# Idle matmuls in the planned waits of TensorE, new task ranks, later weights and last stores by SyncE, in a kernel of gated attention and an MLP

## The chip, the cores and the metric

One core of one Trainium2 chip. The metric is device time in microseconds (us) of one execution of the program, as a median of repeated runs. Engines: PE is TensorE, DVE is VectorE, ACT is ScalarE, POOL is GpSimd, SP is SyncE. The profile's span is counted from the first to the last instruction and is some 1.8 us shorter than the timed run it belongs to.

## The reference

```python
f = 1 / (1 + exp(-f_logit))                      # q, k, v, f_logit: 4 x 8 x 768 x 48, float32
for t in range(S):
    state = f[:, :, t, :, None] * state + k[t] outer v[t]
    y[:, :, t] = q[:, :, t] @ state
x = y as (3072 tokens, 384)
h = x @ w_in                                     # 384 x 2048
out = (h * sigmoid(h)) @ w_out                   # 2048 x 384
```

The kernel works in 24 units: 12 half-chunks m of 128 time steps and two of the four batches, each with two units j. A unit has an attention part (written m.j below) and an MLP part.

## The kernel before

The kernel does not write its instructions in a fixed loop. A small planner inside it holds a list of tasks, each with an engine, an assumed duration, the tasks it needs, a rank and the buffers it takes. It simulates the engines, and the order that comes out is the order in which the instructions are written. Each engine's instruction stream then has that order, with semaphores where the data cross engines. So a constant of the planner can change the order of all five engines. The tasks of a unit, shortened:

```python
add(n("L"),  "ACT", 0.95, logs, ...)          # log of the gate (two ACTIVATEs)
add(n("cs"), "PE",  0.165, cumsum, ...)       # running sum
add(n("ia"), "ACT", 0.4, inverse, ...); add(n("aa"), "ACT", 0.4, forward, ...)
add(n("ki"), "POOL", 1.0, scale_k, ...); add(n("qg"), "DVE", 0.95, scale_q, ...)
add(n("T"),  "PE",  0.45, transposes, ...);  add(n("qk"), "DVE", 0.65, transposed, ...)
add(n("A"),  "PE",  0.34, scores, ...);      add(n("am"), "DVE", 1.25, masked, ...)
add(n("Y"),  "PE",  0.37, outputs, ...);     add(n("yc"), "DVE", 0.5, output_copy, ...)
add(n("D"),  "PE",  0.18, update, ...);      add(n("st"), "DVE", 1.1, state, ...)
add(n("X"),  "PE",  0.17, turn, ...);        add(n("xT"), "DVE", 0.35, turned, ...)
# ... MLP: I (into the hidden layer, PE), S (silu, ACT), O (out, PE), R (copy, ACT), G (store, POOL)
SPLIT = (0, 1, 2)            # half-chunks whose MLP is done per unit, 128 columns a matmul, not 256
BEFORE = {0: ["ki1.0"]}      # the eight weight transfers, issued by POOL, wait for this task
```

The weights are converted from float32 on the way, and POOL issues their transfers. The idle matmuls multiply zeros into an MLP bank of PSUM:

```python
def warm():
    w_ps = hps.tile([128, 2 * HT], F32, name="w_ps", tag="h_ps")
    nc.tensor.matmul(w_ps[:, 0:NP * 2 * D], zeros[:, 0:128], zeros, start=True, stop=True)
# in the planner, before the start of a PE task, while the first MLP task is still to come:
    while start - at > 0.6:
        self.order.append((at, filler)); at += 0.165 if at > 4.5 else 0.33
```

## Time and profile before

| what | before |
|---|---|
| time, median | 204.23 us (203.98 to 205.19, 3 runs) |
| span of the profiled execution | 203.2 us |
| first MLP matmul | 22.25 us |
| PE idle, from there to the last matmul | 6.95 us |
| clock: time lost from there on, (1 - granted clock) x length | 3.3 us (over 60 to 90 us; 3.4 with the rounding of 70 to 78 us) |
| last matmul to the end of the span | 5.1 us |

The last three rows, with the 15.7 us of idle time and idle matmuls before the first MLP matmul, are the budget that the argument uses: time in which PE does nothing useful at full clock. In a stretch of the windows view, idle is length less PE's busy time. The prediction below shows the lines and works the budget out. The profiled execution took 204.98 us.

### The profile page before, as it was taken

The numbers are of one execution on the slowest core, as the hardware profiler recorded it, in microseconds if no ns is written. First come the engines' busy times: TensorE is split into PE (matmuls) and PEld (weight loads), VectorE is DVE, ScalarE is ACT, GpSimd is POOL, SyncE is SP. The second block draws the span as 40 slices with busy tenths as digits, with TensorE's granted clock in tenths as the row PEclk, the third lists the DMA queues.
The fourth block names the chain that finished last, engine by engine and source line by source line (L and its number), as shares of the span: only waits on it lengthen the run. The fifth ranks groups of instructions, "written<-read, shape, count | busy, mean of one in ns | idle before, by whom it ended". The sixth has DMA issues, their size and how long they took to land.

```text
span 203.2 us, 5048 instructions
## 1 busy us (share of the span) xinstructions
PE 186.7 (92%) x2076; PEld 139.1 (68%) x2076; DVE 112.5 (55%) x214; ACT 130.6 (64%) x244; POOL 59.0 (29%) x90
## 2 busy tenths in 40 slices
PE   7788899997999489979999999999999999999990
PEld 3445799554876258658768888667778889865650
DVE  3478650048784956589989940399999750000000
ACT  4446488646898664987798779996346568911110
POOL 5339600135241421192047110473520000012221
PEclk9979999999999959999999999999999999999999
DMA  7999999999999999999999997021110000002111
GB/s 133 187 187 167 170 188 184 197 194 286 189 184 209 214 182 188 180 225 217 175 198 220 205 176 110 2 79 42 39 54 27 3 0 3 0 30 75 68 69 71
DMA packets 105110, 27.06 MB, mean 133 GB/s; under 512 B 100352, under 2 KB 103936, under 8 KB 105088
## 3 DMA queue, kind: packets, MB, share of 16 engines
q1 hardware_dynamic: 99840, 18.88, 58.5%
q0 software_dynamic: 5248, 7.87, 16.2%
q8 instruction: 16, 0.26, 0.6%
q14 instruction: 6, 0.05, 0.1%
HBM read 25.17 MB, written 4.72 MB: 147 GB/s over the span
## 4 chain that ended last, share of the span: by engine, by line
PE 37%; issue 27%; DMA 12%; SPq 9%; DVE 7%; POOL 4%; ACT 2%; POOLq 0%; DVEq 0%; ACTq 0%
PE h_ps L403 14%; DMA q_ld<-in_q_dram 11%; PE o_ps L418 10%; SPq L227 9%; PE t_ps L312 3%; POOL out_dram L432 3%; PE h_ps L388 2%; PE a_ps L324 2%; DVE st L379 2%; DMA f_ld<-in_f_logit_dram 2%; DVE qg L288 2%; POOL ki L285 1%; PE y_ps L344 1%; DVE sd L376 1%; PE y_ps L340 1%
## 5 line engine op out<-in xcount | busy, mean ns | idle before, releaser
L418 PE MATMUL o_ps<-w_out_sb,hT 128*128 128x384 bf16 x384 | 68.4, 326 | 0.4 <-DMA w_out_sb<-in_moe_w_out_dram 0.4
L403 PE MATMUL h_ps<-xT,w_in_sb 128*128 128x256 bf16 x432 | 53.5, 279 | 0.0
L412 ACT ACTIVATE hT<-h_ps 128x512 bf16<-128x512 f32 x72 | 42.8, 597 | 16.3 <-PE h_ps L403 13.7
L418 PEld LDWEIGHTS <-hT 128*128 128x128 bf16 x384 | 36.0, 98 | 22.1 <-issue 0.6
L403 PEld LDWEIGHTS <-w_in_sb 128*128 128x128 bf16 x432 | 41.5, 100 | 6.0 <-issue 0.2
L285 POOL TENSOR_TENSOR ki<-k_ld,ia 128x384 bf16<-128x384 f32 x24 | 24.4, 1018 | 53.5 <-ACT ia L277 41.3
L288 DVE TENSOR_TENSOR qg<-q_ld,a 128x384 bf16<-128x384 f32 x24 | 21.3, 886 | 29.9 <-ACT a L282 18.8
L331 DVE TENSOR_TENSOR atm<-a_ps,triu 128x512 bf16<-128x512 f32 x48 | 30.9, 684 | 7.2 <-PE a_ps L324 6.9
L432 POOL DMA_DIRECT2D out_dram<-o_sb x24 | 13.6, 567 | 57.5 <-ACT o_sb L424 55.1
L424 ACT COPY o_sb<-o_ps 128x384 f32<-128x384 f32 x24 | 11.4, 477 | 23.4 <-PE o_ps L418 23.4
L291 POOL CAST vb<-v_ld 128x384 bf16<-128x384 f32 x22 | 12.9, 593 | 28.8 <-DMA v_ld<-in_v_dram 19.8
L277 ACT ACTIVATE ia<-cs 128x384 f32<-128x384 f32 x24 | 11.8, 492 | 11.4 <-PE cs L272 11.4
L388 PE MATMUL h_ps<-xT,w_in_sb 128*128 128x128 bf16 x288 | 17.7, 219 | 1.3 <-DVE xT L362 0.8
L317 DVE COPY qk<-t_ps 128x1024 bf16<-128x1024 bf16 x24 | 16.4, 682 | 4.4 <-PE t_ps L312 4.4
L258 ACT ACT_TABLE_LOAD x14 | 18.0, 1283 | 1.0 <-PEq L560 0.7
L388 PEld LDWEIGHTS <-w_in_sb 128*128 128x128 bf16 x288 | 16.4, 98 | 2.0 <-issue 1.0
L396 ACT ACTIVATE hT<-h_ps 128x512 bf16<-128x512 f32 x24 | 14.0, 597 | 5.1 <-PE h_ps L388 4.1
L351 DVE CAST y<-y_ps 128x384 bf16<-128x384 f32 x24 | 13.3, 554 | 7.2 <-PE y_ps L344 6.9
L265 ACT ACTIVATE f_ld<-f_ld 128x384 f32<-128x384 f32 x24 | 12.5, 522 | 6.1 <-DMA f_ld<-in_f_logit_dram 6.1
L379 DVE TENSOR_TENSOR st<-sd,al 48x192 bf16<-48x192 f32 x32 | 13.6, 425 | 0.8
L312 PE MATMUL t_ps<-ident,qg 128*128 128x128 bf16 x96 | 9.8, 226 | 3.6 <-DVE qg L288 3.5
L266 ACT ACTIVATE lf<-f_ld 128x384 bf16<-128x384 f32 x24 | 12.5, 523 | 0.8
(41 smaller groups left out, 182.2 us busy)
## 6 DMA issues: line engine op xcount, KB each, us to landing
f_ld<-in_f_logit_dram SPq DMA_DIRECT2D x24, 192.0 KB, 4.5
k_ld<-in_k_dram SPq DMA_DIRECT2D x24, 192.0 KB, 4.6
q_ld<-in_q_dram SPq DMA_DIRECT2D x24, 192.0 KB, 4.5
v_ld<-in_v_dram SPq DMA_DIRECT2D x24, 192.0 KB, 4.7
out_dram<-o_sb POOLq DMA_DIRECT2D x24, 192.0 KB, 2.2
w_in_sb<-in_moe_w_in_dram POOLq DMA_DIRECT2D x4, 384.0 KB, 8.3
w_out_sb<-in_moe_w_out_dram POOLq DMA_DIRECT2D x4, 384.0 KB, 16.4
```

The costliest lines, as they stand in the source:

```text
L227: nc.sync.dma_start(out=t, in_=src)
L258: nc.scalar.preload_act_table_set(tables[name])
L285: nc.gpsimd.tensor_mul(ki[m % 4][:, j, :, 0:D], loaded[m, j, "k"], ias[m, j])
L288: nc.vector.tensor_mul(qg[m % 4][:, j, :, 0:D], loaded[m, j, "q"], aas[m, j])
L317: nc.vector.tensor_copy(qkT[m, j], t_ps[m, j])
L331: nc.vector.tensor_mul(atm[m, j][:, r], att[m, j][:, r], triu[:, None, :].to_broadcast([C, NP, C]))
L379: nc.vector.tensor_mul(st[b][lo:lo + D, :, r * D:(r + 1) * D], src[lo:lo + D, :, r * D:(r + 1) * D], alast[m][lo:lo + D, j, :, None].to_br ...
L388: nc.tensor.matmul(h_ps[:, i], w_in_sb[:, kk, (n + i) * 128:(n + i + 1) * 128], xT[m][:, kk, j], start=(kk == 0), stop=(kk == KT - 1))
L403: nc.tensor.matmul(h_ps[:, i], w_in_sb[:, kk, (n + i) * 128:(n + i + 1) * 128], xT[m][:, kk].rearrange("p b c -> p (b c)"), start=(kk == 0 ...
L412: nc.scalar.activation(hT[m][:, n:n + 2, :], hs[m, n], AF.Silu)
L418: nc.tensor.matmul(os[m, j], hT[m][:, i, j * C:(j + 1) * C], w_out_sb[:, i, :], start=(i == 0), stop=(i == NT - 1))
L432: eng.dma_start(out=out[r0:r0 + C, :], in_=osb[m, j])
```

## The change

The intent is to leave PE without a gap in the plan and to put idle matmuls where a gap remains, so that the clock isn't lowered. The core of the diff:

```diff
-            if e == "PE" and filler is not None and until in left:
+            if e == "PE" and filler is not None:
-                while start - at > 0.6:
+                size, taken = self.pools["h"]
+                while start - at > self.slack:              # slack = 0.4
+                    if len(taken) >= size:
+                        if taken[-size] not in self.freed or self.freed[taken[-size]] > at:
+                            break
                     self.order.append((at, filler))
-    patience = 0.7
+    patience = 2.2
...
-        eng = {"ACT": nc.scalar, "POOL": nc.gpsimd, "SP": nc.sync}[STORE]      # STORE = "POOL"
+        eng = nc.sync if m >= LATE else nc.gpsimd                              # LATE = 8
...
-    SPLIT = (0, 1, 2)
+    SPLIT = (1, 2)
-    BEFORE = {0: ["ki1.0"]}
+    BEFORE = {0: ["ki1.1"], 4: ["ki1.1"]}
...
-            add(n("L"), "ACT", 0.95, ..., rank=r + 5)       # r = m * 10 + j * 3
+            add(n("L"), "ACT", 1.05, ..., rank=base + W["L"])    # base = m * 7 + j * 4
...          # 19 ranks in all, of the attention tasks
-            add(n("qk"), "DVE", 0.65, ...)
+            add(n("qk"), "DVE", 0.68, ...)
-                add(n("D"), "PE", 0.18, ...)
+                add(n("D"), "PE", 0.26, ...)
```

The entry 4 of `BEFORE` adds nothing, as each weight transfer waits for the one before it. Three assumed durations change with the ranks.

More of the change, by code (lines that the diff above doesn't have):

```diff
@@ L72, in pool_ready, with run @@
         return ready
-    def run(self, filler=None, until=None):
+    def run(self, filler=None):
         tasks, end, self.freed = self.tasks, {}, {}
@@ L131, in run @@
                 continue
-            if e == "PE" and filler is not None and until in left:
+            if e == "PE" and filler is not None:
                 at = max(free.get(e, 0.0), 1.0)
-                while start - at > 0.6:
+                size, taken = self.pools["h"]
[3 more added lines that the diff above has]
+                            break
                     self.order.append((at, filler))
                     at += 0.165 if at > 4.5 else 0.33
+                    taken.append(f"warm{at}")
+                    self.freed[f"warm{at}"] = at + 0.2
             if swap:
@@ L176, in allowed @@
         return True
-    patience = 0.7
+    patience = 2.2
+    slack = 0.4
     def emit(self):
@@ L422, in result @@
         osb[m, j] = wk.tile([C, d_model], F32, name="o_sb", bufs=4)
-        if COPY == "ACT":
-            nc.scalar.copy(osb[m, j], os[m, j])
-        else:
-            nc.vector.tensor_copy(osb[m, j], os[m, j])
+        nc.scalar.copy(osb[m, j], os[m, j])
     def store(m, j):
@@ L446, in do @@
         return lambda: fn(*args)
-    COPY, STORE = "ACT", "POOL"
-    SPLIT = (0, 1, 2)
+    W = dict(m=7, j=4, L=1, cs=-2, ia=-9, aa=4, ki=3, qg=1, vb=0, T=5, qk=4, A=3, am=1, Y=14,
+             yc=1, D=13, st=1, X=1, xT=-3, al=5, ea=-1)
+    LATE = 8
+    SPLIT = (1, 2)
     WRANK = -10
-    BEFORE = {0: ["ki1.0"]}
+    BEFORE = {0: ["ki1.1"], 4: ["ki1.1"]}
     units = [(m, j) for m in range(NH) for j in range(HB)]
@@ L464 @@
         g = m // 2
-        add(f"al{m}", "PE", 0.2, do(totals, m), [U("L", m, j) for j in range(HB)], rank=m * 10 + 9, takes="yd", opens=1)
-        add(f"ea{m}", "ACT", 0.18, do(decay_all, m), [f"al{m}"], rank=m * 10 + 1, table="exp", frees=[f"al{m}"], opens=-1)
+        add(f"al{m}", "PE", 0.2, do(totals, m), [U("L", m, j) for j in range(HB)], rank=m * W["m"] + W["al"], takes="yd", opens=1)
+        add(f"ea{m}", "ACT", 0.18, do(decay_all, m), [f"al{m}"], rank=m * W["m"] + W["ea"], table="exp", frees=[f"al{m}"], opens=-1)
         for j in range(HB):
@@ L469 @@
             n = lambda what, mm=m: U(what, mm, j)
-            r = m * 10 + j * 3
+            base = m * W["m"] + j * W["j"]
             back = m >= 4
-            add(n("L"), "ACT", 0.95, do(logs, m, j), [n("f")] + ([n("cs", m - 4), f"al{m - 4}"] if back else []),
-                rank=r + 5, table="exp")
-            add(n("cs"), "PE", 0.165, do(cumsum, m, j), [n("L")], rank=r, takes="yd", opens=1)
-            add(n("ia"), "ACT", 0.4, do(inverse, m, j), [n("cs")], rank=r, table="exp", takes="ia")
@@ L476 @@
-            add(n("aa"), "ACT", 0.4, do(forward, m, j), [n("cs"), n("ia")], rank=r + 1, table="exp", takes="aa", frees=[n("cs")], opens=-1)
+            add(n("L"), "ACT", 1.05, do(logs, m, j), [n("f")] + ([n("cs", m - 4), f"al{m - 4}"] if back else []),
+                rank=base + W["L"], table="exp")
+            add(n("cs"), "PE", 0.165, do(cumsum, m, j), [n("L")], rank=base + W["cs"], takes="yd", opens=1)
+            add(n("ia"), "ACT", 0.4, do(inverse, m, j), [n("cs")], rank=base + W["ia"], table="exp", takes="ia")
@@ L477 @@
+            add(n("aa"), "ACT", 0.4, do(forward, m, j), [n("cs"), n("ia")], rank=base + W["aa"], table="exp", takes="aa", frees=[n("cs")], opens=-1)
             add(n("ki"), "POOL", 1.0, do(scale_k, m, j), [n("ia"), n("k")] + ([n("T", m - 4), n("D", m - 4)] if back and m - 4 < NH - 2 else []),
-                rank=r, frees=[n("ia")])
+                rank=base + W["ki"], frees=[n("ia")])
             add(n("qg"), "DVE", 0.95, do(scale_q, m, j), [n("aa"), n("q")] + ([n("T", m - 4)] if back else []),
-                rank=r + 6, frees=[n("aa")])
+                rank=base + W["qg"], frees=[n("aa")])
@@ L481 @@
             on_act = m == 1
             add(n("vb"), "ACT" if on_act else "POOL", 0.75, do(values_act if on_act else values, m, j), [n("v")] + ([n("Y", m - 4), n("D", m - 4)] if back and m - 4 < NH - 2 else []),
-                rank=r + 1)
-            add(n("T"), "PE", 0.45, do(transposes, m, j), [n("qg"), n("ki")], rank=r + 5, takes="t")
-            add(n("qk"), "DVE", 0.65, do(transposed, m, j), [n("T")], rank=r + 4, takes="qk", frees=[n("T")])
-            add(n("A"), "PE", 0.34, do(scores, m, j), [n("qk")], rank=r + 3, takes="a")
@@ L487 @@
-            add(n("am"), "DVE", 1.25, do(masked, m, j), [n("A")], rank=r + 3, takes="atm", frees=[n("A")])
+                rank=base + W["vb"])
+            add(n("T"), "PE", 0.45, do(transposes, m, j), [n("qg"), n("ki")], rank=base + W["T"], takes="t")
+            add(n("qk"), "DVE", 0.68, do(transposed, m, j), [n("T")], rank=base + W["qk"], takes="qk", frees=[n("T")])
+            add(n("A"), "PE", 0.34, do(scores, m, j), [n("qk")], rank=base + W["A"], takes="a")
+            add(n("am"), "DVE", 1.25, do(masked, m, j), [n("A")], rank=base + W["am"], takes="atm", frees=[n("A")])
@@ L488 @@
             add(n("Y"), "PE", 0.37, do(outputs, m, j), [n("am"), n("vb")] + ([n("st", m - 2)] if m >= 2 else []),
-                rank=r + 2, takes="yd", frees=[n("qk"), n("am")])
-            add(n("yc"), "DVE", 0.5, do(output_copy, m, j), [n("Y")], rank=r + 1, takes="y", frees=[n("Y")])
+                rank=base + W["Y"], takes="yd", frees=[n("qk"), n("am")])
+            add(n("yc"), "DVE", 0.5, do(output_copy, m, j), [n("Y")], rank=base + W["yc"], takes="y", frees=[n("Y")])
             if m < NH - 2:
-                add(n("D"), "PE", 0.18, do(update, m, j), [n("ki"), n("vb"), n("Y"), f"ea{m}"] + ([n("st", m - 2)] if m >= 2 else []),
-                    rank=r + 4, takes="yd")
-                add(n("st"), "DVE", 1.1 if m >= 2 else 0.72, do(state, m, j), [n("D"), n("Y"), f"ea{m}"], rank=r + 3, frees=[n("D")])
@@ L495 @@
-            add(n("X"), "PE", 0.17, do(turn, m, j), [n("yc")], rank=r + 1, takes="yd", frees=[n("yc")])
-            add(n("xT"), "DVE", 0.35, do(turned, m, j), [n("X")], rank=r, frees=[n("X")], takes="xT" if j == 0 else None)
+                add(n("D"), "PE", 0.26, do(update, m, j), [n("ki"), n("vb"), n("Y"), f"ea{m}"] + ([n("st", m - 2)] if m >= 2 else []),
+                    rank=base + W["D"], takes="yd")
+                add(n("st"), "DVE", 1.1 if m >= 2 else 0.72, do(state, m, j), [n("D"), n("Y"), f"ea{m}"], rank=base + W["st"], frees=[n("D")])
@@ L498 @@
+            add(n("X"), "PE", 0.17, do(turn, m, j), [n("yc")], rank=base + W["X"], takes="yd", frees=[n("yc")])
+            add(n("xT"), "DVE", 0.35, do(turned, m, j), [n("X")], rank=base + W["xT"], frees=[n("X")], takes="xT" if j == 0 else None)
         if m in SPLIT:
@@ L521 @@
                     frees=[owner] if n == NT - 4 and j == HB - 1 else None)
-            add(f"R{m}.{j}", COPY, 0.5 if COPY == "ACT" else 0.55, do(result, m, j), [f"O{m}.{j}.{NT - 4}"], rank=-500.0, frees=[f"O{m}.{j}.0"])
-            add(f"G{m}.{j}", STORE, 0.37 if STORE == "ACT" else 0.85, do(store, m, j), [f"R{m}.{j}"], rank=-501.0)
+            add(f"R{m}.{j}", "ACT", 0.5, do(result, m, j), [f"O{m}.{j}.{NT - 4}"], rank=-500.0, frees=[f"O{m}.{j}.0"])
+            add(f"G{m}.{j}", *(("SP", 0.05) if m >= LATE else ("POOL", 0.85)), do(store, m, j), [f"R{m}.{j}"], rank=-501.0)
             add(f"W{m}.{j}", "DMA", 0.6, None, [f"G{m}.{j}"], rank=-1)
@@ L542 @@
         for _ in range(6):
-            plan.run(warm, "I0.0.0" if 0 in SPLIT else "I0.0")
+            plan.run(warm)
             plan.transfers()
```

## The prediction

> **What bounds the kernel now.** I read the engine shares and the 40 slices of the page first, then a table of busy time in stretches cut at the events I found, then the waits of PE after its first MLP matmul, then single stretches of the timeline.
>
> ```profile
> PE 186.7 (92%) x2076; PEld 139.1 (68%) x2076; DVE 112.5 (55%) x214; ACT 130.6 (64%) x244; POOL 59.0 (29%) x90
> ...
> PE   7788899997999489979999999999999999999990
> ...
> PEclk9979999999999959999999999999999999999999
> ```
>
> PE is the bound, but not evenly: the second half is solid and every hole lies in the first 91 us. The clock row has two dips, in the third slice and around the fifteenth. The stretches (PE busy is the first number after the length, the granted clock the seventh field):
>
> ```profile
> 0.00:22.25 22.25, 17.76 (x155) 9.90 (x155) 14.16 (x37) 10.78 (x21) 12.90 (x25) 0.92 1.22 168
> 22.25:41.00 18.75, 18.40 (x262) 15.64 (x263) 4.45 (x11) 13.16 (x22) 2.45 (x3) 1.00 1.23 186
> 41.00:60.00 19.00, 17.30 (x226) 12.57 (x225) 14.13 (x24) 13.93 (x27) 7.57 (x12) 1.00 1.05 213
> 60.00:70.00 10.00, 7.18 (x100) 5.37 (x98) 7.05 (x11) 7.70 (x15) 3.60 (x6) 1.00 1.19 214
> 70.00:78.00 8.00, 7.26 (x63) 5.04 (x61) 4.65 (x10) 4.96 (x9) 1.50 (x2) 0.57 1.07 186
> 78.00:91.00 13.00, 11.69 (x137) 8.42 (x134) 9.42 (x17) 11.06 (x23) 5.66 (x9) 1.00 1.18 194
> 91.00:198.10 107.10, 107.07 (x1153) 82.17 (x1150) 58.65 (x111) 68.53 (x128) 24.82 (x35) 1.00 0.43 86
> 198.10:203.20 5.10, 0.00 (x0) 0.00 (x0) 0.00 (x0) 0.48 (x1) 0.54 (x1) 1.00 0.20 76
> ```
>
> From 91 us on PE is never idle at full clock, so whatever is saved earlier moves the end almost one for one. This gives a budget of the time in which PE does nothing useful at full speed. (a) Before the first MLP matmul at 22.25 us: 4.49 us idle (22.25 - 17.76) and 11.2 us of idle matmuls (the row of line 437), 15.7 us. (b) From 22.25 to 198.1 us: idle 0.35 + 1.70 + 2.82 + 0.74 + 1.31 + 0.03 = 6.95 us. (c) In 70 to 78 us the clock is 0.57, which costs 8.0 x 0.43 = 3.4 us. (d) The tail after the last matmul, 5.1 us. The rest, 203.2 - 31.2 = 172 us, is real work that the change leaves alone.
>
> The holes of (b) have these releasers (waited for: us in total, times, longest):
>
> ```profile
> PE t_ps L312 <- DVE qg L288: 2.5, 2, 2.1
> PE a_ps L324 <- DVE qk L317: 1.3, 1, 1.3
> PE h_ps L388 <- DVE xT L362: 0.8, 1, 0.8
> PE al_ps L300 <- DVE xT L362: 0.7, 1, 0.7
> PE y_ps L340 <- DVE sd L376: 0.6, 1, 0.6
> ```
>
> All are VectorE results of the attention part. VectorE is late because it stood still from 30 to 41 us for want of data:
>
> ```profile
> 40.93 0.56 DVE L288 TENSOR_TENSOR qg<-q_ld,a 128x384 bf16<-128x384 f32 x1 [10.79 <-DMA q_ld<-in_q_dram]
> ```
>
> That q load was issued at 19.35 us and landed 21.5 us later (the median is 4.5): the eight weight transfers, issued by POOL from 16.42 us, took the DMA engines. Afterwards VectorE is only just ahead of PE until 91 us.
>
> **What the Trainium skill says.** "TensorE: Matmul & The Clock Gate", Part 1, states that TensorE runs at half clock until it has been busy for a window of about 3.4 us and falls back after an idle one. The trace agrees: PE is idle for 2.71 of the 4 us between 66 and 70 us, and microsecond slices show 0.50 from 71 to 77, some two windows. "SBUF — State Buffer", Who interferes with whom, states that a VectorE operation with two SBUF inputs and a GpSimd operation block each other. The scaling of q is of that kind, and the trace agrees: 0.54 us at best, 1.90 at worst, here while POOL ran. "ScalarE: Activation LUTs", What ACT_TABLE_LOAD costs, gives about 1283 ns; the trace has 14 at a mean of 1283 ns. "DMA: Bandwidth & Descriptors", Latency and other measured facts, gives a first byte after about 0.6 us for transfers issued by SP and about 1 us for those by POOL; the kernel before has no store issued by SP to compare.
>
> **The change part by part.**
> (1) Idle matmuls no longer stop at the first MLP matmul; they fill every planned PE wait above 0.4 us (before: 0.6) wherever an MLP bank is free in the plan. At full clock one takes about 0.16 us (in the MLP output group, four of the same width take 0.65). They do no work and save none of the idle time itself; they keep the clock. If the holes of (b) are where the plan expects them, the 3.4 us of (c) go. They can also hold a real matmul back by up to one piece each, 0.1 us on average; I allow for five such places, +0.5. As holes stay that the plan does not know, I count -3.0 of the 3.4.
> (2) Weights wait for the key scaling of the last unit of the second chunk (ki1.1) and no longer for ki1.0. In the trace ki1.1 ran at 22.67 only because POOL was issuing weights; its input was there at 19.37. So it ends near 20.4, and the first weight issue moves from 16.42 to about 20.4. The first MLP matmul came 5.8 us after that issue and waited for that weight, so it moves from 22.25 to about 26.2, or +4.0. Meanwhile PE does real work it had to do anyway, the rest of unit 1.1: transposes 0.45, scores 0.33, outputs 0.37, update 0.18, two turns 0.34, about 1.7. Net +2.3. In return four more loads, at 1.0 us each, land at the full rate before the weights take over: one whole unit. VectorE can then work on unit 2.0 while PE does the first 21 us of MLP (4 units of 2.6 + 2.6 us), instead of standing still.
> (3) New ranks and a patience of 2.2 us for changing between the two MLP halves (before 0.7): better order, fewer table loads, and longer planned waits that idle matmuls paper over. Together with (2) this attacks the 6.95 us of (b). Rough supply check: VectorE needs 112.5/24 = 4.7 us a unit, PE 172/24 = 7.2. With one unit in hand VectorE should hardly be caught again. I count 60%, -4.2.
> (4) Stores of the last four chunks go from POOL to SP, which has been idle since 122.4 us. The last store is issued 0.29 us after the copy and takes 0.54 on POOL; POOL is otherwise free there. Only the last store counts: -0.6, an estimate from the 0.54 and the skill's two latencies.
> (5) The first chunk's MLP is no longer split: 256 columns for 128. Twelve narrow matmuls take 0.67 and six wide ones 0.65, so nothing to gain but ScalarE's order.
> Sum: 204.23 + 0.5 - 3.0 + 2.3 - 4.2 - 0.6 = 199.2. I lower it to 198.5: part (2) can cost less, because a warm PE also shortens the attention of the first chunks (in 12.6 to 15.4 us the clock is 0.5 and a scores group takes 0.61 in place of 0.40), so ki1.1 can come sooner.
>
> **Rivals.**
> A: The new order closes nearly all holes. Then (b) and (c) go wholly, 10.3 us, against 2.3 for the late weights and 0.6 at the tail: 195.6. For it: VectorE has 45% idle and 91 to 198 us shows that a full PE is possible. Against it: the plan uses fixed durations, and VectorE's vary from 0.54 to 1.90 us.
> B: The late weights cost as much as they give. The PE order is fixed, so each surprise of a neighbour makes a hole as before; only the clock is kept. Then 204.2 + 0.5 - 3.0 + 2.3 - 1.5 - 0.6 = 201.9. For it: the new ranks come from the plan, whose old ranks also promised fewer holes than the trace shows.
> C: Idle matmuls delay real ones, or wait for a bank that ScalarE has not emptied, and patience leaves real work standing. Forty extra ones of 0.16 us on the path would be 6.4 us and bring 205. Against it: they go only into planned gaps and banks planned free, and any MLP matmul that came next would need a bank too.
>
> **Range and chances.** I predict 198.5 us, between the sum and rival A, with 8 in 10 from 195.0 to 202.3: A at the low end, B within it near the top. Two per cent is at 200.1 us. I give 0.72 to faster, 0.25 to the same, where B or half of B holds, and 0.03 to slower, which needs C.
>
> **What would show it.** (1) Granted clock 1.00 in every slice after the first 16 us; a dip at 60 to 80 us would refute it. (2) First weight issue near 20.4 and first MLP matmul near 26 us; VectorE at work between 27 and 40 us on the third chunk. (3) Real idle time plus idle matmuls after the first MLP matmul under 4 us; if it is 6 or more, the order gained nothing. (4) Last store to end of span under 4 us. The prediction fails if idle matmuls after 26 us outnumber about 30 while PE waits for VectorE as long as before, or if the first MLP matmul is later than 28 us.

## The result and the profile after

The changed kernel took 199.51 us (198.49 to 199.79, 4 runs) against 204.71 us (203.98 to 205.21, 4 runs) for the kernel before; the ratio is 0.974, with a 95% interval of 0.9689 to 0.9791. Ratios here and below are the mean time of one kernel's fast runs over that of the kernel before in fast runs of the same rounds, so they are not quite the ratio of the medians. A second measurement (e12) gave 199.47 us and 0.9757.

From the page of the changed kernel, PE's busy time, the slices of PE and the clock:

```profile
PE 186.5 (94%) x2047; PEld 137.6 (70%) x2047; DVE 112.6 (57%) x214; ACT 128.4 (65%) x242; POOL 55.6 (28%) x82
...
PE   7989879999999999999999989999999999999993
...
PEclk9999999999999999999999999999999999999999
```

Both dips of the clock are gone (the early one is missing in e7 too, so its absence here proves nothing), and the slices after the start are nearly solid. The windows view of the changed kernel, cut at its own first and last MLP matmul (length, PE busy, ..., granted clock, DMA share, GB/s):

```profile
0.00:27.04 27.04, 22.09 (x206) 12.32 (x206) 19.14 (x46) 13.32 (x26) 15.00 (x27) 1.00 1.07 168
27.04:60.00 32.96, 32.46 (x389) 25.31 (x390) 13.45 (x26) 22.43 (x43) 8.71 (x13) 1.00 1.14 197
60.00:70.00 10.00, 9.34 (x143) 7.51 (x141) 8.58 (x17) 8.46 (x15) 2.99 (x6) 1.00 1.01 209
70.00:78.00 8.00, 8.00 (x103) 6.58 (x101) 4.71 (x10) 6.98 (x11) 1.63 (x3) 1.00 1.01 199
78.00:91.00 13.00, 12.77 (x152) 9.61 (x151) 11.04 (x19) 11.95 (x25) 7.39 (x9) 1.00 1.10 206
91.00:194.55 103.55, 101.87 (x1068) 76.31 (x1063) 55.70 (x100) 64.81 (x124) 19.87 (x27) 1.00 0.44 91
194.55:197.90 3.35, 0.00 (x0) 0.00 (x0) 0.00 (x0) 0.48 (x1) 0.00 (x0) 0.98 0.16 61
```

The holes from the first MLP matmul on add up to 0.50 + 0.66 + 0.00 + 0.23 + 1.68 = 3.07 us, against 6.95. The clock loss of 3.4 us is gone, and the tail is 3.35 in place of 5.1. Against that stands the start. Idle time plus idle matmuls before the first MLP matmul were 4.49 + 11.21 = 15.7 us and are now 4.95 + 14.78 = 19.7. The sum, -3.9 - 3.4 - 1.8 + 4.0 = -5.1, compares with the spans' 197.9 - 203.2 = -5.3.

So far this reads like the prediction coming true. The view of the idle matmuls themselves does not (duration in ns, first and last start in us):

```profile
L442 PE MATMUL w_ps<-zeros x63: 322/326/527, 1.1 to 24.7; 128*128 128x384 bf16 x63
```

All 63 lie before the first MLP matmul. Where the clock dip and the holes had been, not one idle matmul runs. The new plan has holes of 0.6 us in all after the first MLP matmul and none above the limit of 0.4, so the new rule finds nothing to fill. I built the changed kernel once with the old limit "only before the first MLP task": all five instruction streams come out the same, instruction for instruction. The part that names the change is empty after 25 us. Something else removed the dip.

### The profile page after: what moved, and what is told of

Same layout as the page of the kernel before. It is cut to its first block, busy times and chain, and to the rows that moved or that the text cites. A ratio compares the mean times of both kernels' runs of the same rounds, so it can differ in the third digit from the quotient of the medians.

```text
span 197.9 us, 4992 instructions
## 1 busy us (share of the span) xinstructions
PE 186.5 (94%) x2047; PEld 137.6 (70%) x2047; DVE 112.6 (57%) x214; ACT 128.4 (65%) x242; POOL 55.6 (28%) x82
## 4 chain that ended last, share of the span: by engine, by line
PE 58%; SPq 23%; DVE 10%; DMA 4%; ACT 2%; issue 1%; ACTq 0%
PE o_ps L426 23%; SPq L235 23%; PE h_ps L411 21%; DMA f_ld<-in_f_logit_dram 4%; PE t_ps L320 3%; DVE atm L339 3%; PE a_ps L332 2%; DVE st L387 2%; DVE qg L296 2%; PE h_ps L396 1%; PE cs L280 1%; PE x_ps L365 1%; DVE y L359 1%; PE y_ps L352 1%; PE y_ps L348 1%
## 5 line engine op out<-in xcount | busy, mean ns | idle before, releaser
L411 PE MATMUL h_ps<-xT,w_in_sb 128*128 128x256 bf16 x480 | 57.5, 273 | 1.4 <-DMA w_in_sb<-in_moe_w_in_dram 1.3
L420 ACT ACTIVATE hT<-h_ps 128x512 bf16<-128x512 f32 x80 | 47.3, 597 | 15.2 <-PE h_ps L411 12.3
L411 PEld LDWEIGHTS <-w_in_sb 128*128 128x128 bf16 x480 | 45.4, 98 | 7.5 <-DMA w_in_sb<-in_moe_w_in_dram 1.4
L426 PEld LDWEIGHTS <-hT 128*128 128x128 bf16 x384 | 35.7, 98 | 20.9 <-issue 0.4
L296 DVE TENSOR_TENSOR qg<-q_ld,a 128x384 bf16<-128x384 f32 x24 | 23.5, 981 | 26.8 <-ACT a L290 25.2
L442 PE MATMUL w_ps<-zeros 128*128 128x384 bf16 x63 | 14.8, 377 | 1.1 <-DVE zeros L541 1.1
L437 POOL DMA_DIRECT2D out_dram<-o_sb x16 | 9.3, 580 | 17.3 <-ACT o_sb L431 14.7
L352 PE MATMUL y_ps<-vb,atm 128*128 128x48 bf16 x192 | 12.2, 184 | 1.1 <-DVE atm L339 0.7
L396 PE MATMUL h_ps<-xT,w_in_sb 128*128 128x128 bf16 x192 | 11.9, 219 | 0.6 <-ACT hT L404 0.6
L352 PEld LDWEIGHTS <-atm 128*128 128x128 bf16 x192 | 9.8, 96 | 3.4 <-DVE atm L339 2.5
L387 DVE TENSOR_TENSOR st<-sd,al 48x192 bf16<-48x192 f32 x32 | 11.5, 360 | 0.8
```

The lines of the kernel that those rows point to most:

```text
L296: nc.vector.tensor_mul(qg[m % 4][:, j, :, 0:D], loaded[m, j, "q"], aas[m, j])
L352: nc.tensor.matmul(y_ps[:, 2 * p + r, :], atm[m, j][:, r, p, :], vb[m % 4][:, j, 2 * p + r, :], start=not opened, stop=True, skip_group_ch ...
L387: nc.vector.tensor_mul(st[b][lo:lo + D, :, r * D:(r + 1) * D], src[lo:lo + D, :, r * D:(r + 1) * D], alast[m][lo:lo + D, j, :, None].to_br ...
L411: nc.tensor.matmul(h_ps[:, i], w_in_sb[:, kk, (n + i) * 128:(n + i + 1) * 128], xT[m][:, kk].rearrange("p b c -> p (b c)"), start=(kk == 0 ...
L420: nc.scalar.activation(hT[m][:, n:n + 2, :], hs[m, n], AF.Silu)
L426: nc.tensor.matmul(os[m, j], hT[m][:, i, j * C:(j + 1) * C], w_out_sb[:, i, :], start=(i == 0), stop=(i == NT - 1))
```

## The experiments

Two theories went in. **Order**: a better order, and first of all the later weights, removes the long holes, and the clock only falls where such a hole is. **Idle matmuls**: they carry the gain, by the clock. The table has what each run left; the profile's numbers are those of its profiled execution. "Holes" is PE idle from the first MLP matmul to the last matmul.

| run | median, us | ratio to before | first MLP matmul | holes | idle matmuls in there, busy us | clock loss in there | tail |
|---|---|---|---|---|---|---|---|
| before | 204.7 | 1 | 22.25 | 6.9 | 0 | 3.3 | 5.1 |
| changed | 199.5 | 0.974 | 27.04 | 3.1 | 0 | 0 | 3.4 |
| e1 late weights only | 204.3 | 1.0013 | 26.09 | 6.0 | 0 | 0 | 5.2 |
| e2 changed, no idle matmuls after 5 us | 199.2 | 0.9768 | 26.42 | 1.8 | 0 | 1.3 | 3.4 |
| e3 changed, all stores by POOL | 200.9 | 0.9838 | 26.67 | 2.5 | 0 | 0 | 5.2 |
| e4 before, new idle matmul rule | 202.7 | 0.9927 | 21.26 | 5.9 | 3.2 | 0 | 5.1 |
| e5 changed, early weights | 203.5 | 0.9937 | 21.62 | 8.3 | 3.3 | 0 | 3.4 |
| e6 changed, old ranks | 199.1 | 0.9711 | 26.86 | 2.6 | 1.8 | 0 | 3.4 |
| e7 before, last stores by SP | 203.3 | 0.9917 | 22.10 | 7.0 | 0 | 3.3 | 3.3 |
| e8 before, new rule up to first MLP task | 205.7 | 1.0038 | 21.35 | 7.7 | 0 | 3.3 | 5.1 |
| e9 e6 with first chunk split | 200.7 | 0.9817 | 27.13 | 4.5 | 0.5 | 0 | 3.4 |
| e10 e6 with old durations | 202.2 | 0.9881 | 26.56 | 4.7 | 2.0 | 0 | 3.3 |
| e11 e6, no idle matmuls after 5 us | 200.0 | 0.9772 | profile slow | | | | |
| e12 changed again | 199.5 | 0.9757 | 26.54 | 2.6 | 0 | 0 | 3.3 |

Results were correct in all twelve runs. e1 to e4 ran on one chip, e5 to e8 on another, e9 to e12 on a third, each against runs of the kernel before on the same chip (medians 204.3, 205.0 and 204.3 us).

### e1: late weights alone

```diff
-    BEFORE = {0: ["ki1.0"]}          # in the kernel before
+    BEFORE = {0: ["ki1.1"]}
```

> The kernel before with one word changed: the weights wait for the key scaling of the last unit of chunk two, as in the changed kernel. Theory Order (the later weights fill the holes after 40 us by letting VectorE start one unit earlier, and with the holes the clock dip goes): first MLP matmul near 26 to 27 us, idle from there to the last matmul at most 4 us, no clock below 0.9 after 30 us, 199.5 to 201.5 us. Theory Idle matmuls (they are what keeps the clock, the order matters little): a dip of the clock remains after 60 us and the time is 203 or more, since the start alone costs 2 us.

204.3 us, ratio 1.0013 (0.9985 to 1.004). Both theories miss. The dip of the clock went, as Order said, but 6.0 us of holes stayed; they only moved. From the windows view of e1, its worst stretch:

```profile
100.00:110.00 10.00, 7.29 (x100) 5.54 (x99) 7.45 (x13) 7.22 (x14) 4.65 (x7) 1.00 1.17 206
```

That stretch was solid before (10.00 of 10 us busy). The timeline of ACT shows one cause: at 100.11 us the gate's logs start after 2.33 us of waiting for a load. The later weights alone gained nothing.

### e2: the changed kernel without idle matmuls

```diff
-                while start - at > self.slack:
+                while start - at > self.slack and at < 5.0:
```

> The changed kernel with its idle matmuls cut to the 14 before 5 us; everything else in the same order. Theory Order: the holes after the first MLP matmul stay as small, but the clock is half at some point between 10 and 30 us and up to 2 us are lost there: 199.5 to 201.5. Theory Idle matmuls: most of the gain goes, 202.5 or more.

199.2 us, ratio 0.9768 (0.9735 to 0.9802), against 0.974 and 0.9757 for the changed kernel: the same, and a little under the 199.5 us at which Order began. Its clock row is the striking one:

```profile
PEclk9855559999999999999999999999999999999999
```

From 8.4 to 28.9 us PE runs at half clock, and nothing is lost. The first MLP matmul comes at 26.42 us, if anything sooner than the 27.04 of the profile with all idle matmuls (26.54 in the second one). The start is paced by loads, with a gate load every 4.2 us, and by the weights, on which PE waits in the changed kernel:

```profile
27.04 1.16 PE L411 MATMUL h_ps<-xT,w_in_sb 128*128 128x256 bf16 x9 [1.28 <-DMA w_in_sb<-in_moe_w_in_dram]
```

### e3: all stores by POOL

```diff
-    LATE = 8
+    LATE = 99
```

> The changed kernel with all stores issued by POOL. The order of PE, VectorE and ScalarE is the same. If the tail is what the store's issuer makes it: the tail from the last matmul to the end of the span goes from 3.35 back to about 5.1 us and the time is 0.7 to 1.8 us longer than the changed kernel. If the tail was shorter for another cause, the time is within 0.4 us.

200.9 us, ratio 0.9838 (0.9808 to 0.9868). The streams of PE, DVE and ACT are the same as in the changed kernel, so the 1% between 0.9838 and 0.974 is the stores. The tail is 5.2 us again. This profile also says that idle matmuls don't guarantee the clock: with all 63 of them PE was idle for 2.23 of the 4 us from 17 on, and the clock was 0.50 from 21 to 24 us. Windows view of e3:

```profile
17.00:21.00 4.00, 1.77 (x22) 1.00 (x22) 1.95 (x4) 2.67 (x7) 1.46 (x2) 0.99 0.87 163
21.00:24.00 3.00, 2.99 (x31) 2.26 (x31) 2.41 (x5) 0.87 (x2) 3.00 (x5) 0.50 1.05 175
```

### e4 and e8: the idle matmul rule alone, in the kernel before

e4 takes the first two hunks of the diff (rule and slack) and leaves weights, ranks, durations and stores alone. Here the rule has holes to fill: 70 idle matmuls, 14 of them after the first MLP matmul. e8 is e4 with the old limit:

```diff
-            if e == "PE" and filler is not None:
+            if e == "PE" and filler is not None and "I0.0.0" in left:
```

> The kernel before with the new rule for idle matmuls alone: 70 in place of 44, of which the plan puts 14 after the first MLP matmul. Theory Idle matmuls: the clock dip after 70 us goes and the time falls by 3 us or more, to 201.3 or less. Theory Order: the real holes at 66 to 70 us come from VectorE and are longer than planned; the time stays within 1.5 us of the kernel before, 203 to 205, and the clock still dips there or PE waits as long.

> The kernel before with the new rule for idle matmuls only up to the first MLP matmul: 56 in place of 44, none later. The run with all 70 had 202.7 us, its first MLP matmul 1.0 us sooner and no clock dip after 70 us. If the gain came from the warm start: the same 202.4 to 203.2. If it came from the 14 later ones, which keep the clock: first MLP matmul near 21.3, but the dip at 70 us is back and the time is 203.3 to 204.5.

e4: 202.7 us, ratio 0.9927 (0.9897 to 0.9958; one of its four runs slow and left out). e8: 205.7 us, ratio 1.0038 (0.9995 to 1.0081), a little slower than the 204.5 us at which I put its upper end. Both bring the first MLP matmul 0.9 to 1.0 us forward. Why is not shown. It isn't the clock: e7, with the PE order and the idle matmuls of the kernel before, had the full clock in its start too, issued its first weights sooner (15.40 us, against 15.96 in e4 and 15.65 in e8), and still had its first MLP matmul at 22.10:

```profile
0.00:22.10 22.10, 16.47 (x155) 9.22 (x155) 14.67 (x38) 10.89 (x21) 13.76 (x26) 1.00 1.18 171
```

e8 shows that this start gains nothing: what PE begins sooner it waits for later, holes 7.7. The dip at 70 us is in e8 and not in e4:

```profile
70.00:78.00 8.00, 7.22 (x60) 5.03 (x58) 4.97 (x10) 4.73 (x9) 1.83 (x3) 0.57 0.94 184
70.00:78.00 8.00, 7.21 (x95) 5.50 (x93) 6.28 (x12) 5.42 (x11) 1.50 (x2) 1.00 0.98 186
```

The first line is e8, the second e4. So in the old order the rule without its old limit is worth about 1.1% (0.9927 against 1.0038), and it works as meant, by the clock. One rival can't be shut out entirely. The rule books an MLP bank for each idle matmul, so e4 differs from e8 by more than the 14: built again, the two plans place a dozen PE tasks, nearly all of the MLP, in another order between 24 and 48 us. But the holes up to 60 us are no smaller in e4 (3.5 us, against 2.7 in e8), so the gain doesn't come from there. Both theories missed e4: Order had it at 203 or more, Idle matmuls at 201.3 or less. It is the changed order that leaves them no work.

### e5 and e6: which of order's two parts

```diff
# e5, in the changed kernel
-    BEFORE = {0: ["ki1.1"], 4: ["ki1.1"]}
+    BEFORE = {0: ["ki1.0"]}
# e6, in the changed kernel: all 19 ranks as before, durations as changed
-                rank=base + W["L"], table="exp")
+                rank=r + 5, table="exp")
...
```

> The changed kernel with the weights again after ki1.0, everything else as changed (12 idle matmuls then fall after the first MLP matmul by plan). First MLP matmul near 21 to 22 us. Theory Pair (neither the ranks nor the late weights gain alone; together they do): holes of 5 us or more return after 40 us, and with the stores on SP the time is 201.5 to 203.5 us. Rival Ranks (the new ranks carry it, the weights' place doesn't matter): 199 to 200.5.

> The changed kernel with the old ranks (weights late, idle matmuls, stores on SP, first chunk not split as changed). Theory Pair: as the run with late weights alone less what the stores gave, 204.3 - 1.5 = 202.8, between 202 and 203.6 us, with holes of 5 us or more after the first MLP matmul. Rival Weights (late weights carry it and something else spoilt that run): under 201.

e5: 203.5 us, ratio 0.9937 (0.9888 to 0.9985), no better than the stores alone (e7). With early weights the new ranks have holes of 8.3 us. e6: 199.1 us, ratio 0.9711 (0.9659 to 0.9762), as fast as the changed kernel. I had expected 202 to 203.6. The theory that ranks and weights are a pair falls: the re-chosen ranks gain nothing that the old ones don't. The late weights are needed (e5, with the new ranks), but e1 had them too, and stood at 1.0013. What e6 has and e1 lacks: stores by SP, the new idle matmul rule, the first half-chunk not split, three durations, and the patience. The patience is out: with the old ranks and with the new the planner gives the same order for 0.7 and 2.2.

### e7: the stores alone

```diff
-        eng = {"ACT": nc.scalar, "POOL": nc.gpsimd, "SP": nc.sync}[STORE]
+        eng = nc.sync if m >= 8 else nc.gpsimd       # in the kernel before
```

> The kernel before with the stores of the last four chunks on SP and nothing else. If the stores gain at the end of the span and nowhere else: tail 3.4 in place of 5.1 us, the time lower by 1.2 to 1.8 us, so 202.5 to 203.1. If the gain in the changed kernel came from a less busy POOL: within 0.5 us of the kernel before.

203.3 us, ratio 0.9917 (0.9858 to 0.9976), tail 3.3 us, holes and dip as before. With e3 this measures the stores twice: about 0.8% and 1.0%, in either order.

### e9 to e12: durations, split, and the changed kernel again

e9 is e6 with `SPLIT = (0, 1, 2)`. e10 is e6 with the old durations (0.95, 0.65, 0.18). e11 is e6 with its idle matmuls cut to the 14 before 5 us. e12 is the changed kernel.

> Late weights, old ranks, stores on SP, with the three re-measured task durations of the change (logs 1.05, transposed copy 0.68, update 0.26) but the first chunk's MLP still split. The run with old ranks had 199.1; late weights alone, less the stores, would be 202.8. Theory Durations (an order planned with truer durations keeps its promise): 198.8 to 200.3. Rival Split: 202 to 203.5. If both share it, about 201.

> The same with the old durations and the first chunk's MLP not split. Theory Split (eight wide tasks with one evacuation each in place of the narrow ones give the better start): 198.8 to 200.3. Rival Durations: 202 to 203.5. The plan itself gives this order 3.5 us more span than the one with the first chunk split, so if the plan were a guide it would be the slowest of the four.

> The run with old ranks, its idle matmuls cut to the 14 before 5 us (63 start ones and 7 later ones become 14 and none). Its order of tasks is the same, and it has neither of the two parts that the change is named for. Theory Order (idle matmuls gain nothing where no long hole is left): 198.6 to 199.6, within 0.5 us of the run with old ranks. Theory Idle matmuls: its seven late ones keep the clock in the holes near 66 to 72 us; without them the clock dips there and it takes 201 or more.

> The changed kernel itself on the same chip, for a comparison with the three others: 199 to 200. If the old ranks are as good, their run without idle matmuls is within 0.5 us of it.

| late weights, old ranks, stores by SP | first chunk split | not split |
|---|---|---|
| old durations | 0.993 (not run: 1.0013 of e1 x 0.9917 of e7) | e10: 0.9881 (0.9856 to 0.9906) |
| new durations | e9: 0.9817 (0.979 to 0.9845) | e6: 0.9711 (0.9659 to 0.9762) |

e9 came out at 200.7 us, just above the range I gave for durations alone and near the 201 that I gave if both share it, e10 at 202.2, in the range where the split alone does little. From old to new durations is 1.1% in the left column and 1.7% in the right; the split is 0.5% above and 1.1% below. The table's new cells come from two chips, and its first cell is a product, so I take the sizes as 1 to 2% for the durations and 0.5 to 1% for the split. (Built again, the product's cell has the order of e1 on PE, ACT and DVE, idle matmuls aside.) Which of the three durations does it was not tried on the chip. The new ones are nearer to the trace of the kernel before (two ACTIVATEs of 0.52 us, 0.68 us, 0.33 us), but that this is why they help is not shown: e10's plan itself has 5.9 us of PE holes after its first MLP matmul, and e6's 3.5. So the planner didn't overlook e10's holes; it happened on a worse order. In plans built without a run, putting any single one of the three back in e6 gives 6.0 to 7.6 us of holes.

e11 was 200.0 us, ratio 0.9772 (0.9745 to 0.98), one of its runs slow and left out; its profile too, so none of its windows are used. It missed what Order expected, 198.6 to 199.6 and within 0.5 us of e6 (199.1 us, on another chip), so e6's idle matmuls after 5 us, seven of them late, may be worth something, 0.6% by the two ratios. e12 was 199.5 us, ratio 0.9757 (0.9731 to 0.9782). So a kernel with neither of the two parts that the change is named for, no idle matmuls after 5 us and no new ranks, is as fast as the changed one within the intervals. No run was clearly faster than the changed kernel.

## Why the prediction was right, and where not

The time, the direction and most of the budget held: 198.5 predicted, 199.2 as the plain sum of its steps, 199.5 measured. The causes held less well, so that the number came out so near is in part luck: step 3's gain came from another cause, and the start cost more than forecast while the tail gained more.

**Step 1, idle matmuls.** Predicted -3.0 for the clock and +0.5 for matmuls held back. The clock loss of 3.3 us went, but this is the step that failed: it was not the idle matmuls that removed it. No idle matmul runs after 24.7 us, e2 without them is as fast, and e1 lost the dip with the old rule. The clock fell after PE had been idle for 2.71 of 4 us; with that hole gone it stayed (e1). The step's mechanism is seen at work in the old order (e4 against e8, 1.1%, with the rival named there). I had assumed that the new plan would still have holes to fill; it has 0.6 us.

**Step 2, late weights.** The first weight issue was predicted at 20.4 us and came at 20.10; the first MLP matmul at 26.2, and came at 27.04 and 26.54, as the first weights took longer to land. The net cost of the start was a term of +2.3; idle time and idle matmuls there rose by 4.0; against e7, whose start has the old PE order at full clock (5.63 us idle and 10.54 of idle matmuls), by 3.6. The 0.7 us that I took off the sum for a warmer start has no support: e2, at half clock there, issued its first weights at 20.48 us and was as fast. The return was half as described. DVE works on the third half-chunk from 29.8 to 35.8 us, where it had stood since 30.1. Then it stands still again, for as long as before, one unit further on:

```profile
46.57 0.69 DVE L296 TENSOR_TENSOR qg<-q_ld,a 128x384 bf16<-128x384 f32 x1 [10.76 <-ACT a L290]
```

It no longer waits for a load directly but for ACT, which is in its run of silu activations until 42.7 us, then changes tables and takes up the gates. So the late weights don't cure the standstill; they put one unit in hand in front of it. e5 shows that this unit matters: without it 8.3 us of holes.

**Step 3, ranks and patience.** Predicted -4.2 for the holes; measured 6.95 to 3.07, or -3.9. The size is right and the cause is wrong. The ranks are worth nothing that shows (e6), the patience doesn't alter the program. Late weights are worth about 2% in the changed kernel (0.974 and 0.9757, against 0.9937 with early weights in e5) and nothing in e1. What makes the difference, with the old ranks, is the durations, which I did not count at all, and the split, of which step 5 says that there is "nothing to gain but ScalarE's order". A plan made with a logs task of 0.95 us and an update of 0.18 us put its holes at 2.2 us, and the chip made 6.0 of them (e1). Of e1's distance to e6, 4.7 us of span, the holes explain 3.4 and the tail 1.8, and the start takes 0.8 back; PE's busy time after the first MLP matmul is nearly the same, 165.08 and 164.82 us. The 1.79 us of e6's late idle matmuls are not a cost of that size: by the records of the trace, a real matmul is under way in all but 0.8 us of them.

**Step 4, stores.** The mechanism was right and the term mis-sized: -0.6 predicted, -1.8 us measured in the tail, 1.4 us (e3, against the changed kernel in other rounds) and 1.7 us (e7) in the medians. From the end of the last copy to the first bytes it fell from 1.4 to about 0.9 us. The other 1.2 us I had not foreseen: after its last bytes the span goes on for 2.5 us when POOL issued the store (e3 as well) and for 1.3 us when SP did (1.2 in e7). The DMA views of the last microseconds, 40 slices of 0.25 us from 194.0, before and after:

```profile
GB/s 0 0 0 295 369 123 0 0 0 0 0 0 0 0 0 0 295 369 123 0 0 0 0 0 387 313 86 0 0 0 0 0 0 0 0 0 0 0 0 0
```

```profile
GB/s 326 381 80 0 0 0 0 43 369 350 25 0 0 0 0 0 0 0 0 0 0 0 0 0 0 0 0 0 0 0 0 0 0 0 0 0 0 0 0 0
```

By the DMA records, which are finer than these slices: before, the copy ended at 198.63, the data run from 200.05 to 200.72 and the span ends at 203.2. After, the copy ended at 195.10, the data run from 195.96 to 196.63 and the span ends at 197.9.

**Rivals.** A, all holes closed, was nearest in its mechanism; 3 us of holes are left. B, the late weights give nothing, is what e1 shows; with the old ranks and the old durations e10 took 202.2 us, near B's 201.9. The new ranks with the old durations were not tried. C, idle matmuls in the way, did not happen: in the changed kernel there are none where PE is the bound.

**The signs I named.** The clock at 1.00 and the holes under 4 us came true, and I would have read both as proof of the steps I had named. Counting where the idle matmuls start, one line of one view, was what showed otherwise.

**A reading of the skill.** By "SBUF — State Buffer", Who interferes with whom, the prediction lets any GpSimd operation block a VectorE operation with two SBUF inputs. The page says so only of a GpSimd operation that reads SBUF, and the trace agrees with the page: beside a scaling of k the scaling of q took up to 1.90 us, but at 16.66 us, while POOL issued weights, it took 0.55.

## What to carry to other kernels

Before crediting a part of a change with a gain, look whether its instructions run where the gain is. A planner's order can hang on small differences in its assumed durations: changes of 0.03 to 0.1 us in three of them moved this kernel by 1 to 2%, while 19 re-chosen ranks moved it by nothing that shows, and the plan's own span did not rank the variants (191.9 us for e9 and 193.6 for e6, of which e6 is the faster on the chip). Keeping the clock up paid where PE was the bound (e4 against e8, 1.1%); in a start paced by loads, half the clock cost nothing (e2, 199.2 us).

## What the Trainium skill lacked or had wrong

- "TensorE: Matmul & The Clock Gate", HAM oscillation, puts the rule as no idle gaps above some 3.4 us (the section after it lets micro-idles do it too, without a measure). Here the clock fell after much shorter ones: the longest single gap before the dip at 70 us was 2.06 us, with PE idle for 2.71 of 4 us. The prediction called this agreement. In the changed kernel the clock came through a gap of 1.28 us at 27 us. The clock record changes in steps of 3.41 us. In five profiles (e11, slow, left out) it fell after a step in which PE was busy for 37 to 52% (e2 at 8.4 us 1.25 us, before at 70.3 us 1.35, e7 1.46, e8 1.57, e3 at 20.9 us 1.77 of 3.41 us), and at full clock it came through every step with 56% or more (1.92 us in e8 from 87.54 us on; 2.01 and 2.04 in a row in e5 from 66.51 us on), but for one: before, at 12.24 us, it fell after 66% (2.27 us), where e7 came through with 71%. So here the busy share of a step tells better than the longest gap, with one case against it. The page's Terms also give the penalty of a low clock as its time by (1 - K/N). In this start that is no measure of the cost: in e2 it comes to 26.42 x 0.34 = 9.0 us in the start, and the time didn't change (199.2 us against 199.5).
- "DMA: Bandwidth & Descriptors", Latency and other measured facts, has about 0.4 us between the first bytes of SP's and POOL's transfers. For a last store the difference was 1.8 us in the span: 0.6 from the end of the copy until the data moved (of which 0.3 lies between the start of the issue and the first bytes, 1.13 and 0.84 us), and 1.2 from the last bytes to the end. A difference by issuer in that last stretch no page has.
